# Attention and two MLPs on one core: Q loaded in one transfer per tile, two V tiles issued by ScalarE, another order, last flips in halves

## The chip, the cores and the metric

The kernel runs on one core of one Trainium2 chip. The metric is the device time of one execution in microseconds. PE is TensorE, DVE is VectorE, ACT is ScalarE, POOL is GpSimd, and SP is SyncE, which here only issues transfers. A transfer issued by SP or by ACT is an instruction in that engine's own queue.

## What is computed

Chunked attention with memory keys, then two MLPs, all in float32, each product of the MLPs split in a high and a low part so that it takes three matmuls:

```python
# q, k, v: batch 4, 8 heads, 768 positions, 64 wide; chunks of 32, left 16, right 8, 8 memory keys
for c in range(nc):
    k_full = np.concatenate([mem_k, k_ctx], axis=2)
    v_full = np.concatenate([mem_v, v_ctx], axis=2)
    scores = scale * np.matmul(q_c, k_full.transpose(0, 1, 3, 2))
    scores = scores - np.max(scores, axis=-1, keepdims=True)
    a = np.exp(scores)
    a = a / (np.sum(a, axis=-1, keepdims=True) + 1e-09)
    out[:, :, c_start:c_end] = np.matmul(a, v_full)
...
h = x @ w_in;  g = softplus(h);                                x = g @ w_out      # 3072 x 512, 2048 wide
h = x @ w_in;  g = np.maximum(h, 0) + alpha * np.minimum(h, 0); y = g @ w_out     # the second MLP
```

The weights of both MLPs arrive as doubles and are made float32 on the chip.

## The kernel before

There are 24 attention tiles of 128 tokens. A tile t goes through these steps, named as the planner names them: load Q and K (`load_q`, `load_k`) and V (`load_v`, six transfers); order Q by chunk on ACT (`qo`, `qp`, function `a_order`); copy the memory keys on POOL (`km`); scores on PE (`s`); maximum on DVE (`m`); subtract it (`c`, function `a_shift`) and exponential on ACT (`e`); sum, reciprocal on DVE (`n`, `r`); multiply by the reciprocal (`w`, on POOL for the first tiles); transpose on PE (`t`); copy the turned tile on ACT (`pt`); values on PE (`v*`); high and low half of x on ACT and DVE (`xh`, `xl`). Four tiles make one block of 512 tokens.

The first MLP goes over the six blocks in segments; one step of it is `h` (12 matmuls into `ps_hh`), softplus, high and low half, `out` (12 matmuls into `ps_o`). A pair of raw weight tiles per column group is loaded (`raw`, three buffers), made float32 by five DVE operations (`ab`, `cl`, `ca`, `cb`, `cv`), and split on ACT and POOL or DVE (`wh`, `wl`). The second MLP works on three pairs of blocks by a scheme of seven products (`quad`, `second`); its results are turned by DVE in 32x32 blocks and stored (`flip`), the very last quarter by PE (`ending`, `turn`).

The order of everything up to the second MLP comes from `Plan`: pieces with an engine, a length, a due time and what they come after. `schedule` adds the pieces; the table `O` holds offsets of the due times and switches; the plan of eight rounds that ends first by its own lengths is written out, so that each engine's queue is fixed when the program is built. `keep_busy` puts matmuls on a tile of zeros ahead of those PE pieces for which the plan sees PE idle.

In the kernel before each of the first eight tiles takes Q in two transfers, one for each half of the partitions, and only the halves of the rows that hold data; the other halves of the target (`s_room`) are set to zero by `others` (piece `qz`, four memsets, on POOL, for tile 0 on DVE). All V are issued by SP. Two lines set this:

```python
sp.dma_start(out=raw_q[t][part].rearrange("p (n k) -> p n k", k=D), in_=rows)        # load_q, for e in 0, 1
(dve.tensor_copy if other else act.copy)(out=own(q_t[t], e), in_=raw_q[t][e * D:(e + 1) * D]...)   # a_order
```

Two forms of the shifted exponential stand in the kernel already: `a_shift` with `a_exp` (DVE subtracts 512 columns, ACT takes one exponential of 512), and `a_bias` with `a_shifted_exp` (DVE scales the 8 maxima, ACT takes eight exponentials of 64 columns, each with its own bias). The switches `ca0` (tiles 0 to 3) and `ca1` (tiles 4 to 7) choose the second when they are above 0.5.

Of the kernel before, what the change touches and what calls it, by code (L numbers as in the profile page):

```python
# [31 lines left out]
QN = 2 * NPAIR * P  # L32
# [48 lines left out]

PLAN = []
RUNS = 8
O = {'qo': 19.43, 'km': 103.61, 's': 132.4, 'm': 86.98, 'c': -51.87, 'e': 175.6, 'n': -19.49, 'r': -46.35, 'w': -19.52, 't': 95.77, 'pt': 85.42, 'v': 4.11, 'xh': -85.13, 'xl': -37.52, 'first': 4.43, 'gap': 13.49, 'second': 13.8, 'gap2': 10.89, 'raw': 76.14, 'ab': -97.97, 'cl': -24.77, 'ca': -41.63, 'cb': -28.14, 'cc': -52.39, 'wh': 1.69, 'wl': -37.29, 'odd': 61.8, 'sp': 29.0, 'hi': -84.66, 'lo': 120.66, 'out': 14.22, 'wait': 0.06, 'sloads': 10.35, 'qo0': 31.77, 'qo1': 59.63, 'km0': 45.44, 'km1': -1.09, 's0': 33.53, 's1': 68.06, 'm0': 99.26, 'm1': -29.86, 'c0': 87.42, 'c1': 86.99, 'e0': -47.46, 'e1': 46.23, 'n0': 20.17, 'n1': -4.91, 'r0': 23.19, 'r1': -6.49, 'w0': -81.15, 'w1': -23.28, 't0': 107.79, 't1': -40.96, 'pt0': 0.74, 'pt1': -5.53, 'v0': -87.68, 'v1': 71.52, 'xh0': -18.53, 'xh1': -22.32, 'xl0': 2.53, 'xl1': 34.49, 'by0': 3.34, 'by1': 1.01, 'va': -80.0, 'vb': -248.8, 'vc': -188.24, 'vd': -121.62, 'ra': -92.44, 'rb': -99.39, 'rc': -59.46, 'wld': -3.93, 'dra': -16.84, 'qpd': -4.87, 'ca0': 0.43, 'ca1': -2.85}


class Plan:
# [16 lines left out]
    def run(self):  # L104
# [10 lines left out]
        while left:  # L115
            able, first = [], 1e9
            for name, since in ready.items():
                engine, us, due, _, _, take, _, _ = left[name]
                t = max(since, free.get(engine, 0.0) if engine else 0.0, now)
                if engine == "SP":  # L120
                    t = max(t, free.get("DMA", 0.0) - 4.0)
                for r in set(take):
                    short = take.count(r) - rooms[r]
                    if short > 0:
                        later = sorted(u for u, g in back if g == r)
                        t = max(t, later[short - 1] + self.LAG if len(later) >= short else 1e9)
# [24 lines left out]
            for u, g in [x for x in back if x[0] <= t]:  # L151
                rooms[g] += 1
                back.remove((u, g))
            if tab and tab != table:
                us, table = us + 1.3, tab
            if engine == "PE":
                if self.beside(name) and self.beside(last_pe):
                    us -= 0.24
                last_pe = name
                if t < 90.0 and t - free.get("PE", 0.0) > 0.5:  # L160
                    self.idle[name] = (max(free.get("PE", 0.0), came), t)
            if engine == "DVE" and free.get("POOL", 0.0) > t:
                us += 0.25 * min(us, free["POOL"] - t)
# [13 lines left out]
def attention_mlp_mlp_kernel(ctx: ExitStack, tc, qk, v, w1, w2, consts, out):  # L177
# [605 lines left out]
    def second(p, todo):  # L783
# [34 lines left out]
        for n in range(7 * NQ):  # L818
# [88 lines left out]
    def schedule(when):  # L907
# [5 lines left out]
        def nothing():  # L913
            pass

        def dma(name, issue, move, due, work, after=(), take=(), give=(), eng="SP"):
            add(("i",) + name, eng, issue, due, work, after, take)
            add(("x",) + name, "DMA", move, due, nothing, [("i",) + name])
            add(name, "", 2.0, due, nothing, [("x",) + name], [], give)

        for n, k in enumerate(order):
            f = k // 2
# [12 lines left out]
        for i, (b, f, first, final) in enumerate(steps):  # L935
# [10 lines left out]
            if final:  # L946
# [5 lines left out]
                for m in range(4):  # L952
                    by_act = m % 2 == 0 or f < HALF and O["dra"] > 0.5
                    add(("dr", i, m), "ACT" if by_act else "DVE", 0.65, t + 12.6, lambda i=i, m=m, b=b, by_act=by_act: drain_one(0 if by_act else 1, acc[b][m], staged[i][:, m, :]), [("db", i)], [], ["acc"])
                    dma(("dd", i, m), 1.1 if adds else 0.4, 1.0 if adds else 0.8, t + 16, lambda i=i, m=m, b=b, adds=adds: drain_to(m, staged[i][:, m, :], b, adds),
                        [("dr", i, m)], eng="POOL" if adds else "SP")
                add(("ds", i), "", 0.0, 0, nothing, [("dd", i, m) for m in range(4)], [], room if f < HALF else [])


# [6 lines left out]
        def tile(t, prev, due, step=None):  # L966
# [214 lines left out]
```

## Time and profile before

| | us |
|---|---|
| median of 3 runs (lowest, highest) | 1090.9 (1090.0, 1092.84) |
| the profiled execution | 1089.11 |
| its span | 1087.1 |
| PE busy | 1066.3 (98%) |
| DVE, ACT, POOL busy | 717.6, 559.7, 232.9 |

The profiled execution stands 1.8 us below the median. PE is busy through nearly all of the span, but busy time counts the matmuls on zeros too (43 of them, all before 65 us), and the matmuls of the first 72 us are spread between waits. After 72 us PE waits once, for 0.7 us, until the end of the last product at 1081 us; then come the last turns and stores.

### The profile page before, as it was taken

The numbers are of one execution on the slowest core, as the hardware profiler recorded it, in microseconds if no ns is written. First come the engines' busy times: TensorE is split into PE (matmuls) and PEld (weight loads), VectorE is DVE, ScalarE is ACT, GpSimd is POOL, SyncE is SP. The second block draws the span as 40 slices with busy tenths as digits, with TensorE's granted clock in tenths as the row PEclk, the third lists the DMA queues.
The fourth block names the chain that finished last, engine by engine and source line by source line (L and its number), as shares of the span: only waits on it lengthen the run. The fifth ranks groups of instructions, "written<-read, shape, count | busy, mean of one in ns | idle before, by whom it ended". The sixth has DMA issues, their size and how long they took to land.

```text
span 1087.1 us, 16452 instructions
## 1 busy us (share of the span) xinstructions
PE 1066.3 (98%) x6003; PEld 874.6 (80%) x6003; DVE 717.6 (66%) x1150; ACT 559.7 (51%) x974; POOL 232.9 (21%) x281
## 2 busy tenths in 40 slices
PE   7799999999999999999999999999999999999998
PEld 4578878888888888888888888888888888888886
DVE  6799989566644544444358166778666779666976
ACT  5654335465563554353244355765455665456543
POOL 4444444424123332223233400000000000000000
PEclk9899999999999999999999999999999999999999
DMA  9955674768644465444356373799874999856904
GB/s 225 234 152 185 167 187 121 187 164 215 186 127 151 153 197 137 167 118 151 111 194 225 134 304 113 293 276 318 201 275 174 335 300 255 239 223 252 370 1 78
DMA packets 173839, 214.53 MB, mean 197 GB/s; under 512 B 96064, under 2 KB 125888, under 8 KB 166848
## 3 DMA queue, kind: packets, MB, share of 16 engines
q1 hardware_dynamic: 169456, 196.59, 56.6%
q0 software_dynamic: 4032, 16.78, 7.9%
q8 instruction: 47, 0.77, 0.3%
q14 instruction: 32, 0.26, 0.1%
q10 hardware_dynamic: 272, 0.13, 0.0%
HBM read 154.74 MB, written 46.14 MB: 185 GB/s over the span
## 4 chain that ended last, share of the span: by engine, by line
PE 94%; DVE 3%; DMA 2%; SPq 1%; ACT 0%; issue 0%; DVEq 0%; ACTq 0%
PE ps_q L71 41%; PE ps_o L71 24%; PE ps_hh L71 24%; PE ps_x L71 2%; PE ps_s L71 2%; DVE word L71 1%; DMA raw<-in_w_dram 1%; PE ps_t L71 1%; SPq L71 1%; DMA wout<-out_ops 1%; DMA qk<-in_qk_dram 0%; DVE sm L71 0%; DVE x L71 0%; DVE nm L71 0%; DVE v L71 0%
## 5 line engine op out<-in xcount | busy, mean ns | idle before, releaser
L71 PE MATMUL ps_hh<-x,wsplit 128*128 128x512 f32 x1152 | 280.2, 392 | 0.6 <-DVE x L71 0.5
L71 PE MATMUL ps_o<-g,wsplit 128*128 128x512 f32 x1152 | 279.4, 391 | 0.8 <-ACT ta L71 0.7
L71 PEld LDWEIGHTS ps_o<-g,wsplit 128*128 128x128 f32 x1152 | 215.0, 188 | 46.5 <-ACT ta L71 1.1
L71 PEld LDWEIGHTS ps_hh<-x,wsplit 128*128 128x128 f32 x1152 | 214.5, 188 | 45.7 <-DVE x L71 0.8
L71 PE MATMUL ps_q<-g,wout 128*128 128x512 f32 x1008 | 229.3, 389 | 0.1
L71 PE MATMUL ps_q<-xop,win 128*128 128x512 f32 x1008 | 229.2, 389 | 0.0
L71 PEld LDWEIGHTS ps_q<-g,wout 128*128 128x128 f32 x1008 | 189.1, 188 | 39.8 <-ACT gb L71 0.5
L71 PEld LDWEIGHTS ps_q<-xop,win 128*128 128x128 f32 x1008 | 189.2, 188 | 39.4
L71 DVE TENSOR_TENSOR g<-ta,g 128x512 fp32r<-128x512 f32 x96 | 71.8, 748 | 132.3 <-ACT g L71 132.1
L71 ACT CAST g<-gb 128x512 fp32r<-128x512 f32 x168 | 100.8, 622 | 88.5 <-PE ps_q L71 64.6
L71 DVE TENSOR_TENSOR g<-gb,g 128x512 fp32r<-128x512 f32 x168 | 114.3, 687 | 37.9 <-ACT g L71 36.2
L71 ACT CAST g<-ta 128x512 fp32r<-128x512 f32 x96 | 59.6, 621 | 147.8 <-PE ps_o L71 147.6
L71 ACT ACTIVATE ta<-ps_hh 128x512 f32<-128x512 f32 x96 | 57.4, 598 | 106.3 <-PE ps_hh L71 101.9
L71 DVE SCALAR_TENSOR_TENSOR word<-raw,word 128x512 int32<-128x512 int32 x128 | 106.3, 831 | 2.5
L71 ACT ACTIVATE tp<-gb 128x512 f32<-128x512 f32 x48 | 30.4, 633 | 91.8 <-DVE gb L71 91.8
L71 POOL TENSOR_TENSOR wst<-wsum,wst 128x512 fp32r<-128x512 f32 x32 | 42.3, 1321 | 124.6 <-ACT wst L71 124.6
L71 POOL DMA_DIRECT2D gb<-gb x12 | 10.5, 874 | 263.6 <-DVE g L71 176.1
L71 DVE TENSOR_SCALAR word<-word 128x512 f32<-128x512 f32 (+1 forms) x128 | 65.0, 512 | 1.8
L71 POOL TENSOR_TENSOR wsplit<-word,wsplit 128x512 fp32r<-128x512 f32 x32 | 48.9, 1531 | 64.7 <-ACT wsplit L71 58.1
L71 DVE SCALAR_TENSOR_TENSOR gb<-gb,tp 128x512 f32<-128x512 f32 x48 | 33.2, 692 | 44.0 <-ACT tp L71 44.0
L71 POOL TENSOR_TENSOR wst<-word,wst 128x512 fp32r<-128x512 f32 (+1 forms) x32 | 37.6, 1176 | 110.7 <-ACT wst L71 110.7
L71 DVE TENSOR_SCALAR word<-raw 128x512 int32<-128x512 int32 x64 | 39.0, 610 | 32.0 <-POOL wst L71 13.6
(81 smaller groups left out, 930.9 us busy)
## 6 DMA issues: line engine op xcount, KB each, us to landing
wout<-out_ops SPq DMA_DIRECT2D x42, 1024.0 KB
raw<-in_w_dram SPq DMA_DIRECT2D x64, 512.0 KB
win<-in_ops SPq DMA_DIRECT2D x24, 1024.0 KB
win<-in_ops SPq DMA_DIRECT2D x24, 768.0 KB
out_ops<-wst SPq DMA_DIRECT2D x56, 256.0 KB
in_ops<-wst SPq DMA_DIRECT2D x24, 512.0 KB
gb<-gb POOLq DMA_DIRECT2D x12, 1024.0 KB, 13.5
v<-in_v_dram SPq DMA_DIRECT2D x48, 128.0 KB
```

Of the source, the lines that this page charges most:

```text
L71: i = getattr(self.engine, name)(*args, **kw)
```

## The change

Q of the first eight tiles comes in one transfer of 128 rows of 4 KB, zeros included (the host's layout holds them), so the memsets `qz` are gone; `a_order` copies all 128 partitions for one chunk at a time. `load_v` takes a queue, and the switches `vq0` and `vq4` put V of tiles 0 and 4 on ACT's queue. The table `O` is another one throughout (cut below to the switches that change what is done: `ca0` is now on, `wld` puts the low halves of the first two weight tiles on DVE, all `by` stay on). `Plan` weighs DVE, PE and accumulating transfers a little differently, which moves pieces but is no work. The flip of the quarter (0, 0) of each pair comes at steps 50 and 51, one half at each, where both halves came at step 53; the other two flips stay at steps 39 and 46.

```diff
-O = {... 'wld': -3.93, 'dra': -16.84, 'qpd': -4.87, 'ca0': 0.43, 'ca1': -2.85}
+O = {... 'wld': 2, 'dra': 0, 'qpd': 0, 'ca0': 1, 'ca1': 0, 'vq0': 1, 'vq1': 0, 'vq2': 0, 'vq3': 0, 'vq4': 1, 'vq5': 0, 'vq6': 0, 'vq7': 0, 've': 70.11}
...
-            raw_q[t] = room[:, :QN // 2]
+            raw_q[t] = room[:, :QN]
...
         if c is None:
-            sp.dma_start(out=raw_q[t][part].rearrange("p (n k) -> p n k", k=D), in_=rows)
+            sp.dma_start(out=raw_q[t], in_=qk[t][:, :QN])
...
-    def load_v(t):
+    def load_v(t, queue):
...
-            sp.dma_start(out=v_t[t][to:to + n, part], in_=v[t][at:at + n, part])
+            queue.dma_start(out=v_t[t][to:to + n, part], in_=v[t][at:at + n, part])
 
     def a_order(t, e, other=False):
-        (dve.tensor_copy if other else act.copy)(out=own(q_t[t], e), in_=raw_q[t][e * D:(e + 1) * D].rearrange("p (n c k) -> p c n k", c=2, k=CHUNK))
+        (dve.tensor_copy if other else act.copy)(out=q_t[t][:, e], in_=raw_q[t].rearrange("p (n c k) -> p c n k", c=2, k=CHUNK)[:, e])
...
-            if (i, q) in ((4, 7), (5, 6), (6, 5)):
-                d, b = ((0, 1), (1, 1), (0, 0))[i - 4]
-                flip(c.pop((d, b)), 2 * p + b, d)
+            for at, half, d, b in ((39, 0, 0, 1), (39, 1, 0, 1), (46, 0, 1, 1), (46, 1, 1, 1), (50, 0, 0, 0), (51, 1, 0, 0)):
+                if n == at:
+                    flip(c[d, b], 2 * p + b, d, [half])
...
-                add(("qz", t), "POOL" if t else "DVE", 1.5 if t else 1.1, (-50, 0)[t > 0] + t, lambda: others(q_t[t], pool if t else dve), [("vr", t)])
```

The order. First place: the head of ACT's queue. `v_119`, `v_117` hold tile 0's V and ordered Q, `qk_97` to `qk_100` tiles 0 to 3's Q and K; DMAHW0 to 7 are eight semaphores that the transfers of SP and ACT take in turn, so that a transfer waits in its queue until the one that held its semaphore before has landed. Before:

```order
L71 ACT_TABLE_LOAD
L71 COPY v_119<-qk_97 64x16x32 [waits DMAHW0_49]
L71 COPY v_119<-qk_97 64x16x32 [waits DMAHW1_49]
L71 COPY v_171<-qk_98 64x16x32 [waits DMAHW3_49]
L71 ACTIVATE v_119<-v_119 128x512 [waits DVE_49,PE_49]
L71 COPY v_171<-qk_98 64x16x32 [waits DMAHW4_49]
```

And in the changed kernel:

```order
L71 DMA v_117<-in_v_dram 8x512
L71 DMA v_117<-in_v_dram 56x512
L71 DMA v_117<-in_v_dram 64x512
L71 DMA v_117<-in_v_dram 64x512 [waits DMAHW1_49]
L71 DMA v_117<-in_v_dram 56x512 [waits DMAHW3_49]
L71 DMA v_117<-in_v_dram 8x512 [waits DMAHW5_49]
L71 ACT_TABLE_LOAD
L71 COPY v_117<-qk_97 128x512 [waits DMAHW0_49]
L71 COPY v_117<-qk_97 128x512
L71 COPY v_129<-qk_98 128x512 [waits DMAHW2_49]
L71 COPY v_129<-qk_98 128x512
L71 ACTIVATE v_117<-ps_s,nm 128x64 [waits DVE_49,PE_49,Activation_49]
```

The six transfers of V now stand ahead of everything that ACT does; the fourth waits for DMAHW1, which tile 0's K (`qk_97`, 128x4x160) holds, the fifth and sixth for V's own first and second piece.

Second place: SP's queue behind the V of tile 3 (`v_255`, in the changed kernel `v_216`). Before, tile 4's Q and K (`qk_340`) and V (`v_357`) follow, then tile 5's Q (`qk_358`):

```order
L71 DMA v_255<-in_v_dram 56x512 [waits DMAHW6_49]
L71 DMA v_255<-in_v_dram 8x512 [waits DMAHW7_49]
L71 DMA qk_340<-in_qk_dram 64x8x64 [waits DMAHW0_49]
L71 DMA qk_340<-in_qk_dram 64x8x64 [waits DMAHW1_49]
L71 DMA qk_340<-in_qk_dram 128x4x160 [waits DMAHW2_49]
L71 DMA v_357<-in_v_dram 8x512 [waits DMAHW3_49]
```

In the changed kernel two weight tiles come first, the second of which (the fourth in all) waits for DVE to free one of the three raw buffers, and Q and K of tiles 4 to 7 follow without V:

```order
L71 DMA raw<-in_w_dram 128x512 [waits DMAHW3_49]
L71 DMA raw<-in_w_dram 128x512 [waits DMAHW4_49,DVE_49]
L71 DMA qk_392<-in_qk_dram 128x1024 [waits DMAHW5_49]
L71 DMA qk_392<-in_qk_dram 128x4x160 [waits DMAHW6_49]
L71 DMA qk_421<-in_qk_dram 128x1024 [waits DMAHW7_49]
L71 DMA qk_421<-in_qk_dram 128x4x160 [waits DMAHW0_49]
L71 DMA qk_441<-in_qk_dram 128x1024 [waits DMAHW2_49]
```

Third place: ACT behind the turned copy of tile 2 (`pt`). Before, weights (`wsplit`), x of tile 2 and Q of tile 4 follow:

```order
L71 COPY pt<-ps_t 64x8x32 x3
L71 CAST wsplit<-word 128x512 [waits DVE_49]
L71 CAST x<-ps_x 128x4x128 [waits PE_49]
L71 COPY v_357<-qk_340 64x16x32 [waits DMAHW0_49]
L71 COPY pt_95<-ps_t 64x8x32 [waits PE_49,Activation_49]
L71 COPY pt_95<-ps_t 64x8x32 [waits Activation_49] x3
```

In the changed kernel tile 3's exponentials and tile 4's V stand ahead of x of tile 2 and of everything of tile 3 behind its exponential:

```order
L71 CAST wsplit<-word 128x512 [waits DVE_49]
L71 ACTIVATE v_216<-ps_s,nm 128x64 x7
L71 DMA v_422<-in_v_dram 8x512 [waits DMAHW1_49]
L71 DMA v_422<-in_v_dram 56x512 [waits DMAHW3_49]
L71 DMA v_422<-in_v_dram 64x512 [waits DMAHW5_49]
L71 DMA v_422<-in_v_dram 64x512 [waits DMAHW7_49]
L71 DMA v_422<-in_v_dram 56x512 [waits DMAHW1_49]
L71 DMA v_422<-in_v_dram 8x512 [waits DMAHW3_49]
L71 CAST wsplit<-word 128x512 [waits DVE_49]
L71 CAST x<-ps_x 128x4x128 [waits PE_49]
L71 COPY pt_95<-ps_t 64x8x32 [waits PE_49]
```

Here DMAHW5 was last taken by Q of tile 4 (`qk_392`, 128x1024) and DMAHW7 by Q of tile 5 (`qk_421`, 128x1024).

## Rows read from the trace of the kernel before

**Rows 1.** Windows: length, PE, PEld, DVE, ACT, POOL busy (instructions), PEclk, DMA share, GB/s.

```profile
20.00:30.00 10.00, 7.60 (x93) 4.55 (x89) 9.86 (x20) 6.19 (x14) 5.65 (x11) 1.00 0.93 264
...
40.00:50.00 10.00, 6.34 (x74) 5.30 (x73) 7.15 (x17) 6.08 (x11) 1.98 (x4) 0.66 0.97 243
...
200.00:300.00 100.00, 100.00 (x724) 82.81 (x723) 60.06 (x98) 54.78 (x93) 34.43 (x44) 1.00 0.72 191
```

**Rows 2.** Waits of PE from 72 us on: in total, times, longest.

```profile
PE ps_o L71 <- ACT ta L71: 0.7, 1, 0.7
```

**Rows 3.** The chain that ended last, near 83 us: start, length, what.

```profile
83.02 2.72 PE ps_hh L71 x12
```

**Rows 4.** PE in order of time: start, length, operation, [idle before <- releaser].

```profile
1.01 4.84 PE L71 MATMUL ps_s<-zero 128*128 128x512 bf16 x11 [1.01 <-POOL zero L71]
6.51 1.17 PE L71 MATMUL ps_s<-qk,v 128*64 128x64 f32 x32 [0.67 <-POOL qk L71]
...
34.20 2.83 PE L71 MATMUL ps_hh<-x,wsplit 128*128 128x512 f32 x11 [0.54 <-DVE x L71]
...
44.47 1.11 PE L71 MATMUL ps_t<-cst,v 128*128 128x128 f32 x4 [3.39 <-POOL v L71]
45.86 1.98 PE L71 MATMUL ps_s<-qk,v 128*64 128x64 f32 x32 [0.27 <-DVE v L71]
47.59 1.95 PE L71 MATMUL ps_x<-pt,v 128*64 128x64 f32 x32
...
55.33 0.60 PE L71 MATMUL ps_t<-cst,v 128*128 128x128 f32 x4
...
58.63 1.15 PE L71 MATMUL ps_x<-pt,v 128*64 128x64 f32 x32
```

**Rows 5.** SP's queue in the opening: start, time to issue, transfers.

```profile
0.75 4.06 SPq L71 DMA_DIRECT2D qk<-in_qk_dram  x6
...
9.66 3.04 SPq L71 DMA_DIRECT2D v<-in_v_dram  x6
...
25.38 2.21 SPq L71 DMA_DIRECT2D qk<-in_qk_dram  x3
```

**Rows 6.** ACT in the opening, columns as rows 4.

```profile
0.75 1.28 ACT L71 ACT_TABLE_LOAD   x1 [0.75 <-PEq L1171]
3.82 0.62 ACT L71 COPY v<-qk 64x512 f32<-64x512 f32 x1 [1.79 <-DMA qk<-in_qk_dram]
...
15.19 1.51 ACT L71 COPY pt<-ps_t 64x256 f32<-64x256 f32 x4 [3.12 <-PE ps_t L71]
```

**Rows 7.** POOL in the opening, columns as rows 4.

```profile
6.25 0.36 POOL L71 COPY qk<-qk 128x32 f32<-128x32 f32 x2 [4.21 <-DMA qk<-in_qk_dram]
```

**Rows 8.** DVE in the opening, columns as rows 4.

```profile
18.18 0.43 DVE L71 TENSOR_SCALAR word<-raw 128x512 int32<-128x512 int32 x1 [0.20 <-DMA raw<-in_w_dram]
18.52 0.68 DVE L71 TENSOR_REDUCE sm<-v 128x8 f32<-128x512 f32 x1
...
22.31 0.20 DVE L71 RECIPROCAL r<-sm 128x8 f32<-128x8 f32 x1
...
24.42 0.67 DVE L71 SCALAR_TENSOR_TENSOR word<-raw,word 128x512 int32<-128x512 int32 x1
```

**Rows 9.** Short windows, columns as rows 1: Q alone, then weights alone.

```profile
2.50:3.00 0.50, 0.50 (x2) 0.15 (x1) 0.41 (x2) 0.00 (x0) 0.00 (x0) 1.00 0.87 198
...
64.00:65.00 1.00, 1.00 (x12) 0.61 (x9) 0.17 (x1) 0.79 (x2) 1.00 (x1) 1.00 0.94 385
```

**Rows 10.** SP's queue at the end, columns as rows 5.

```profile
1078.64 4.15 SPq L71 DMA_DIRECT2D out_dram<-c  x8
1082.89 1.05 SPq L71 DMA_DIRECT2D out_dram<-o_sb  x2
```

**Rows 11.** ACT at the end: its copies, then its one transfer.

```profile
1081.89 0.89 ACT L71 COPY o_sb<-ps_q 128x512 f32<-128x512 f32 x2 [4.74 <-PE ps_q L71]
1082.81 0.49 ACTq L71 DMA_DIRECT2D out_dram<-o_sb  x1
```

More of the change, by code (lines that the diff above doesn't have):

```diff
@@ L83 @@
 RUNS = 8
-O = {'qo': 19.43, 'km': 103.61, 's': 132.4, 'm': 86.98, 'c': -51.87, 'e': 175.6, 'n': -19.49, 'r': -46.35, 'w': -19.52, 't': 95.77, 'pt': 85.42, 'v': 4.11, 'xh': -85.13, 'xl': -37.52, 'first': 4.43, 'gap': 13.49, 'second': 13.8, 'gap2': 10.89, 'raw': 76.14, 'ab': -97.97, 'cl': -24.77, 'ca': -41.63, 'cb': -28.14, 'cc': -52.39, 'wh': 1.69, 'wl': -37.29, 'odd': 61.8, 'sp': 29.0, 'hi': -84.66, 'lo': 120.66, 'out': 14.22, 'wait': 0.06, 'sloads': 10.35, 'qo0': 31.77, 'qo1': 59.63, 'km0': 45.44, 'km1': -1.09, 's0': 33.53, 's1': 68.06, 'm0': 99.26, 'm1': -29.86, 'c0': 87.42, 'c1': 86.99, 'e0': -47.46, 'e1': 46.23, 'n0': 20.17, 'n1': -4.91, 'r0': 23.19, 'r1': -6.49, 'w0': -81.15, 'w1': -23.28, 't0': 107.79, 't1': -40.96, 'pt0': 0.74, 'pt1': -5.53, 'v0': -87.68, 'v1': 71.52, 'xh0': -18.53, 'xh1': -22.32, 'xl0': 2.53, 'xl1': 34.49, 'by0': 3.34, 'by1': 1.01, 'va': -80.0, 'vb': -248.8, 'vc': -188.24, 'vd': -121.62, 'ra': -92.44, 'rb': -99.39, 'rc': -59.46, 'wld': -3.93, 'dra': -16.84, 'qpd': -4.87, 'ca0': 0.43, 'ca1': -2.85}
+O = {'qo': 30.33, 'km': 84.14, 's': 91.95, 'm': 109.26, 'c': -17.61, 'e': 178.31, 'n': -17.92, 'r': -11.95, 'w': -78.56, 't': 180.11, 'pt': 161.35, 'v': 22.95, 'xh': -41.96, 'xl': 4.27, 'first': 21.85, 'gap': 34.28, 'second': 0.0, 'gap2': 0.83, 'raw': 107.43, 'ab': -164.05, 'cl': 0.38, 'ca': -84.0, 'cb': -2.76, 'cc': -13.13, 'wh': -66.22, 'wl': -41.75, 'odd': 77.78, 'sp': 86.94, 'hi': -161.87, 'lo': 79.15, 'out': 7.77, 'wait': 0.1, 'sloads': 35.53, 'qo0': -11.74, 'qo1': 136.15, 'km0': 35.59, 'km1': 41.17, 's0': 26.73, 's1': 74.58, 'm0': 133.68, 'm1': -93.99, 'c0': 162.97, 'c1': 149.24, 'e0': -109.85, 'e1': 67.1, 'n0': 14.44, 'n1': -56.97, 'r0': -9.69, 'r1': 13.43, 'w0': -135.29, 'w1': -76.5, 't0': 138.51, 't1': -5.69, 'pt0': -54.64, 'pt1': 57.94, 'v0': -156.16, 'v1': 16.61, 'xh0': -36.76, 'xh1': -159.4, 'xl0': -11.13, 'xl1': 106.59, 'by0': 1, 'by1': 1, 'va': -84.93, 'vb': -183.48, 'vc': -136.3, 'vd': -247.55, 'ra': -159.88, 'rb': -94.86, 'rc': -102.4, 'wld': 2, 'dra': 0, 'qpd': 0, 'ca0': 1, 'ca1': 0, 'vq0': 1, 'vq1': 0, 'vq2': 0, 'vq3': 0, 'vq4': 1, 'vq5': 0, 'vq6': 0, 'vq7': 0, 've': 70.11}
 class Plan:
@@ L159, in run @@
                 last_pe = name
+                if t > 90.0 and t - free.get("PE", 0.0) > 2.0:
+                    us += 1.6
                 if t < 90.0 and t - free.get("PE", 0.0) > 0.5:
                     self.idle[name] = (max(free.get("PE", 0.0), came), t)
-            if engine == "DVE" and free.get("POOL", 0.0) > t:
-                us += 0.25 * min(us, free["POOL"] - t)
+            if engine == "DVE":
+                us *= 0.88
+                if free.get("POOL", 0.0) > t:
+                    us += 0.3 * min(us, free["POOL"] - t)
             done[name] = t + us
@@ L767, in ending, with flip @@
             turn(c[:, 1, part], 1, 2 * h, 2, (lambda o, i: act.copy(out=o, in_=i), dve.tensor_copy)[h], (act, sp)[h])
-    def flip(c, b, d):
+    def flip(c, b, d, halves=range(2)):
         rows = out[b * N2:(b + 1) * N2, d * HK:(d + 1) * HK].rearrange("(c i) (m a j) -> m a i c j", i=32, m=2, j=32)
-        for m in range(2):
+        for m in halves:
             o = c[:, m, :].rearrange("p (c i) -> p c i", i=32)
@@ L914, in nothing, with dma @@
             pass
-        def dma(name, issue, move, due, work, after=(), take=(), give=(), eng="SP"):
+        def dma(name, issue, move, due, work, after=(), take=(), give=(), eng="SP", land=2.0):
             add(("i",) + name, eng, issue, due, work, after, take)
             add(("x",) + name, "DMA", move, due, nothing, [("i",) + name])
-            add(name, "", 2.0, due, nothing, [("x",) + name], [], give)
+            add(name, "", land, due, nothing, [("x",) + name], [], give)
         for n, k in enumerate(order):
@@ L954, in schedule @@
                     add(("dr", i, m), "ACT" if by_act else "DVE", 0.65, t + 12.6, lambda i=i, m=m, b=b, by_act=by_act: drain_one(0 if by_act else 1, acc[b][m], staged[i][:, m, :]), [("db", i)], [], ["acc"])
-                    dma(("dd", i, m), 1.1 if adds else 0.4, 1.0 if adds else 0.8, t + 16, lambda i=i, m=m, b=b, adds=adds: drain_to(m, staged[i][:, m, :], b, adds),
-                        [("dr", i, m)], eng="POOL" if adds else "SP")
+                    dma(("dd", i, m), 1.2 if adds else 0.4, 2.2 if adds else 0.8, t + 16, lambda i=i, m=m, b=b, adds=adds: drain_to(m, staged[i][:, m, :], b, adds),
+                        [("dr", i, m)], eng="POOL" if adds else "SP", land=4.0 if adds else 2.0)
                 add(("ds", i), "", 0.0, 0, nothing, [("dd", i, m) for m in range(4)], [], room if f < HALF else [])
@@ L981, in load @@
             def load(c=None):
-                for e in range(2):
+                for e in range(2 if few else 1):
                     load_q(t, e, c)
@@ L987, in tile @@
             else:
-                dma(("qk", t, 2), 1.45, 2.7, soon, lambda: (load(), load_k(t)), [("qr", t)])
+                dma(("qk", t, 2), 1.2, 2.9, soon, lambda: (load(), load_k(t)), [("qr", t)])
             kafter = [("i", "q", t, 1)]
@@ L992, in tile @@
             add(("vr", t), "", 0.0, soon + 2, lambda: room_v(t), [("i", "qk", t, 2)] + ([("i", "v", prev)] if prev >= 0 else []), vrooms)
-            dma(("v", t), 2.9, 2.0, (O["va"], O["vb"], O["vc"], O["vd"])[t] if start else due - 24, lambda: load_v(t), [("vr", t)])
+            by_act = not few and O["vq%d" % t] > 0.5
+            dma(("v", t), 3.0, 2.0, (O["va"], O["vb"], O["vc"], O["vd"])[t] if start else due - (24 if few else O["ve"]), lambda: load_v(t, act if by_act else sp), [("vr", t)], eng="ACT" if by_act else "SP")
             queries = [("q", t, c) for c in range(2) if few or c]
             if not few:
-                add(("qz", t), "POOL" if t else "DVE", 1.5 if t else 1.1, (-50, 0)[t > 0] + t, lambda: others(q_t[t], pool if t else dve), [("vr", t)])
-                add(("qo", t), "ACT", 0.6, due - when_due("qo"), lambda: a_order(t, 0), [("qk", t, 2), ("qz", t)])
+                add(("qo", t), "ACT", 0.6, due - when_due("qo"), lambda: a_order(t, 0), [("qk", t, 2), ("vr", t)])
                 other = start and O["qpd"] > 0.5
-                add(("qp", t), "DVE" if other else "ACT", 0.5 if other else 0.6, due - when_due("qo"), lambda: a_order(t, 1, other), [("qo", t)])
+                add(("qp", t), "DVE" if other else "ACT", 0.7 if other else 0.6, due - when_due("qo"), lambda: a_order(t, 1, other), [("qo", t)])
                 queries = [("qp", t)]
```

## The prediction, written before the changed kernel ran

> **What bounds the kernel now.** I read the windows first, then PE's waits, then PE, ACT, POOL, DVE and SP in order of time. From 72 us on PE waits once, for 0.7 us [rows 2], and a stage such as 200 to 300 us is full of matmuls [rows 1]. Nothing off PE can be won there. What can move is when PE gets there. I use a mark: by 83.02 us [rows 3] the kernel before has finished the scores, transposes and values of tiles 0 to 7 and ten products of the first MLP (six `h`, four `out`), each 2.72 us [rows 3]. The changed order has the same PE work behind it after seven `h` and three `out`. If the mark comes x us later, the end does too, as long as the rest stays full.
>
> Up to the mark PE is not full: it waits 3.39 us for POOL before 44.47 [rows 4], and the mean granted clock from 40 to 50 us is 0.66 [rows 1], that is, the lower level, 1.2 GHz, for much of it, after that wait. A score step takes 1.98 us there and 1.17 at 2.4 GHz, a transpose 1.11 and 0.60, values 1.95 and 1.15 [rows 4]. The transfers are as full as PE is not: DMA share 0.93 and 0.97 [rows 1]. So the opening is a race between loads and a chain of ACT, DVE and POOL steps, and the first `h` at 34.20 [rows 4] is where it is read.
>
> **Transfers of Q.** Before, a tile's Q is 262 KB in short rows; such a stretch moved 198 GB/s [rows 9], 1.3 us. Now it is 524 KB in rows of 4 KB; weights in rows of that length moved 385 GB/s [rows 9], 1.4 us. I take 1.4: twice the bytes in about the same time. The far bound is the mean of a mixed stretch, 264 [rows 1]: 2.0 us. SP issues one transfer less, some 0.7 us per tile (three took 2.21 [rows 5], the last of them K).
>
> **The memsets** of POOL and DVE go. In PE's waits for POOL they stand behind the scores of tile 1; what they give is covered by step 1 below, which is later. I count nothing. The shift of tiles 0 to 3 leaves DVE (one tensor operation of about 0.7) for ACT: eight exponentials of 64 columns for one of 512. Nothing in the trace is that small on ACT; four copies of 256 columns took 1.51, 0.38 each, one of 512 took 0.62 [rows 6], and the line through them gives 0.20, 1.6 us a tile (1.2 if the fixed part is smaller, 2.0 if the bias adds).
>
> **Two V on ACT.** SP needs 3.04 us to issue a V [rows 5]. If SP's issuing were the limit, two V less would free 6.1 us. But the share of the DMA engines in that stretch is 0.93 to 0.97 [rows 1], so the bytes are the limit and I count no gain. The Trainium skill, "DMA: Bandwidth & Descriptors", section "Issuing engines are not separate DMA queues", says the same against the change: transfers started by several engines run on the same 16 DMA engines, and only issue time is saved. By that rule the move is worth at most those 6.1 us and here nothing; the DMA share agrees.
>
> What the move costs is ACT. A transfer in ACT's queue holds ACT until its semaphore is free, and behind it stand the table load and every copy. The trace of before has no such wait, so I walk through the order.
>
> *Step 1, the head.* ACT's fourth piece of V waits for tile 0's K. K landed by 6.25 before [rows 7]. Ahead of it now are 0.1 us more of Q and the first three pieces of V, 262 KB at 264 GB/s [rows 1], 1.0 us: 7.3 (6.3 if V gets no share, 8.3 if all 524 KB more go at 264). Three issues at 0.49 [rows 11] make 8.8, the table load 1.28 and two copies of 0.62 [rows 6] make 11.3, the scores 1.17 make 12.5. PE's filler ends at 5.85 [rows 4] and nothing follows until about 11, so I expect the lower level, 0.8 more: 13.3, where before it was 7.68.
>
> *Step 2, tiles 0 to 2.* Maximum 0.68 and scaling 0.20 [rows 8] bring the first exponential to 14.3. From there ACT runs nearly without a break: 1.6, Q of tile 2 1.24, 1.6, turned copy 1.51, half of Q of tile 3 0.62, 1.6, and 0.5 of waiting for the transpose: 23.0. DVE then has a sum 0.68, a low half of x 0.7, scaling and reciprocal 0.20 each: 24.8. Only then comes the first weight tile's conversion, three operations of 0.43 and two of 0.67 [rows 8]: 27.4. It frees the raw buffer for the fourth weight tile, and **Q and K of tiles 4 to 7 stand behind that transfer on SP**. Tile 4's Q, issued at 25.38 before [rows 5], goes out at 27.8.
>
> *Step 3, tile 4's V.* ACT's fourth piece waits for tile 5's Q. From issue at 0.75 [rows 5] to ACT's copy at 3.82 [rows 6] the first half of Q took 3.07 us, of which 0.7 was moving 131 KB at 198: 2.4 fixed. In front are a weight tile and two Q at 385, 4.1 us, a K of 328 KB at 264, 1.2, and three pieces of V, 1.0: it lands at 36.1 (38.0 with everything at 264). Three issues: 37.6. Before, ACT waited for no load of this kind.
>
> *Step 4, the first `h`.* ACT: weights and x of tile 2, 1.24; turned copy of tile 3, 1.51; Q of tile 4, 1.24; weights and half a Q, 1.24; high half of x of tile 3, 0.6; DVE's low half 0.7, behind another operation of 0.7: 44.8, **10.6 us later** than 34.20.
>
> *Step 5, from there to the mark.* By then the scores of tiles 4 and 5 are done. Left: ten products 27.2, two scores 2.3, four transposes 2.4, four values 4.6, together 36.5 at 2.4 GHz, if PE is full: the weights are converted, V of tiles 5 to 7 are issued from about 41 on, and DVE, 9.86 of 10 busy in rows 1, has spent its idle time earlier. That gives 81.3. The kernel before needs 48.8 us for its part, since it waits. PE again idled before 39 us, so one transpose, score and values cost up to 2.1 more [rows 4]; half of it lies under ACT's copies of step 4: 1.0. These sums leave out the hand-overs between engines: POOL's first copy of two ends at 6.43 [rows 7] and PE begins at 6.51 [rows 4], 0.08. For some twenty I add 1.5. The mark is at 83.8, **0.8 us late**.
>
> **The halves of the last flip.** SP issues the last eight stores of `c` until 1082.79 and the two turned results right behind, though the first copy that they wait for began at 1081.89 and took about 0.6 [rows 10, 11]. Two to three steps earlier (six matmuls each, half a product, 1.36 us) SP is free: 0.4 us gained (0 if the last store's landing sets the end anyway, 1.0 if its bytes also wait less). DVE's two transposes fall between its low halves for PE, which the code asks for three steps ahead (`asked`), 4 us; that covers them, and without it each would cost PE its own length.
>
> **Sum.** 1089.11 + 0.8 - 0.4 = 1089.5 against the profiled execution; the median of before stands 1.8 above it, so 1091.3. Within 0.3% (3.3 us either way, about what a measurement of this kernel can tell from no change) is 1087.6 to 1094.2, and that is this case's own range. Chance 0.54.
>
> **Rival: ACT isn't held.** If tile 4's and 5's Q have landed when ACT comes to tile 4's V, that costs only six issues, 2.9 us. ACT comes there at about 30.6 (23.0, then 0.6, 1.51, 0.62, 0.6, 1.51, 0.62, 1.6 and 0.5 of waits) and leaves at 33.5 instead of 37.6: 4.1 us won. If the head isn't held either, another 4 us at the first score, of which the loads give back half: 1091.3 - 6.1 = 1085.2. For it speaks that SP needs only some 2 us to issue Q and K of tiles 4 and 5; against it that 1.6 MB and more would have to move in the 3 us behind the fourth weight tile. Decides: tile 5's Q landed before 31 us. Chance 0.20.
>
> **Rival, slower: long rows go no faster than the mix.** If Q moves at 264 and not 385 GB/s, eight tiles take 4.8 us more of a full DMA stretch: 0.7 at the head, 1.3 in step 3, and the rest on tiles 6 and 7 and the V behind them, before which PE would wait. With a PE that waits for those in full (1.5 of the remaining 2.8) and the other half of the low clock in step 5 (1.0) it makes 4.5: 1095.8. The point from which it is slower than 0.3% is about 290 GB/s. For it: K, Q, V and weights lie mixed in these queues, and the mixed mean is 264. Chance 0.26.
>
> **Chances and range.** Faster by over 0.3%: 0.20, within: 0.54, slower: 0.26, the three cases. Half of each rival lies outside 1086 to 1096, under 0.2 together.
>
> **What would show it.** Right: ACT's first copy of Q near 10 us, a wait of ACT on a load of Q ending near 36, the first `h` near 45, and PE full from there to the mark near 83.8. Wrong: the first `h` before 40 (ACT not held), PE waits between 45 and 83 of over 2 us (loads late), or waits of over 1 us after 90, which no step here has.

## The result, and the profile after

The changed kernel takes 1096.7 us (median of 6, 1095.6 to 1097.5) where the kernel before took 1090.95 in the same session (median of 6): a ratio of 1.0051, interval 1.004 to 1.0062, 5.7 us slower. The prediction of 1091.3 and its range to 1096 were too low. The profiled execution is 1095.6 us long, its span 1093.8.

Up to the mark the prediction held; the loss lies behind it. First the head and the middle of ACT's opening in the changed kernel (start, length, operation, [idle before <- releaser]); rows 6 show the head before:

```profile
0.74 7.18 ACTq L71 DMA_DIRECT2D v<-in_v_dram  x6
7.96 1.28 ACT L71 ACT_TABLE_LOAD   x1 [7.96 <-DMA v<-in_v_dram]
9.26 2.18 ACT L71 COPY v<-qk 128x512 f32<-128x512 f32 x4
...
33.36 4.81 ACTq L71 DMA_DIRECT2D v<-in_v_dram  x4
38.20 0.62 ACT L71 CAST wsplit<-word 128x512 fp32r<-128x512 f32 x1 [5.91 <-DMA v<-in_v_dram]
```

ACT issues V of tile 0 until 7.92 and the last four pieces of tile 4's V until 38.17, and nothing of its own runs meanwhile. PE of the changed kernel, same columns; the counterparts before are rows 4:

```profile
40.01 1.98 PE L71 MATMUL ps_x<-pt,v 128*64 128x64 f32 x32 [3.39 <-ACT pt L71]
...
45.70 3.37 PE L71 MATMUL ps_hh<-x,wsplit 128*128 128x512 f32 x12
...
83.69 2.88 PE L71 MATMUL ps_o<-g,wsplit 128*128 128x512 f32 x12
86.42 2.88 PE L71 MATMUL ps_hh<-x,wsplit 128*128 128x512 f32 x12
...
108.98 2.88 PE L71 MATMUL ps_hh<-x,wsplit 128*128 128x512 f32 x12
114.31 4.58 PE L71 MATMUL ps_o<-g,wsplit 128*128 128x512 f32 x12 [2.44 <-DVE o_sb L71]
...
138.65 2.97 PE L71 MATMUL ps_o<-g,wsplit 128*128 128x512 f32 x12 [0.68 <-DVE o_sb L71]
```

The mark of the kernel before, in the same columns:

```profile
82.86 2.88 PE L71 MATMUL ps_hh<-x,wsplit 128*128 128x512 f32 x12
```

The first `h` starts at 45.70 and the mark (seven `h`, three `out` done) is at 83.69, 0.8 behind the kernel before, where it is at 82.86 in this view and 83.02 in rows 3. The product that starts at 138.65 is the 19th from the mark on; eighteen products at 2.72 are 49.0 us, and here they took 55.0. So of the 6.5 us between the two profiled executions 0.8 come up to the mark and 6.0 behind it; the kernel before has one wait of 0.7 further on, at 152 us, that the changed kernel doesn't have. PE's waits from 72 us on, in total, times, longest; rows 2 had 0.7 in one wait:

```profile
PE ps_o L71 <- DVE o_sb L71: 3.6, 3, 2.4
```

The waits are for DVE's copies of `ps_o` (the odd `dr` pieces), which free the accumulator banks; behind the longest of them the next 12 matmuls took 4.58 instead of 2.88, 1.7 more, at a granted clock of 0.79 from 114 to 116 us and 0.57 from 116 to 119. Together with the waits that is 5.3 of the 6.0 us. Three windows (0 to 80, 80 to 84, 84 to 140), columns as rows 1, first of the kernel before, a stretch that rows 1 left out:

```profile
0.00:80.00 80.00, 64.59 (x695) 47.24 (x696) 61.97 (x120) 47.69 (x88) 35.20 (x72) 0.94 0.79 207
80.00:84.00 4.00, 4.00 (x20) 3.30 (x19) 4.00 (x8) 1.82 (x4) 1.35 (x1) 1.00 0.41 131
84.00:140.00 56.00, 55.87 (x247) 45.99 (x246) 55.69 (x83) 22.35 (x40) 25.70 (x18) 1.00 0.62 179
```

and of the changed kernel:

```profile
0.00:80.00 80.00, 65.14 (x686) 47.92 (x691) 57.62 (x115) 49.64 (x115) 22.12 (x42) 0.89 0.81 226
80.00:84.00 4.00, 4.00 (x20) 3.30 (x19) 3.97 (x6) 1.63 (x4) 4.00 (x2) 1.00 0.83 228
84.00:140.00 56.00, 52.36 (x222) 42.24 (x221) 55.24 (x84) 21.32 (x37) 21.67 (x17) 0.97 0.54 164
```

DVE (third pair) was busy 55.69 of 56 us in the kernel before already, beside a PE that was full by itself: two engines at their limit at once, with no slack for DVE. The chain by line between 40 and 139 us changes accordingly, first before, then after:

```profile
by line: PE ps_hh L71 39.9%; PE ps_o L71 36.2%; DMA raw<-in_w_dram 5.1%; PE ps_x L71 4.3%; DVE word L71 3.3%; DVE sm L71 3.1%; PE ps_t L71 2.6%; PE ps_s L71 2.0%; ACT pt L71 1.5%; DVE nm L71 1.4%; issue 1.3%; DVE v L71 1.3%; DVE r L71 0.6%;
```

```profile
by line: DVE word L71 59.0%; issue 13.7%; DVE g L71 7.5%; PE ps_hh L71 5.8%; DVE o_sb L71 2.6%; DVE x L71 2.5%; PE ps_s L71 2.2%; ACT pt L71 1.5%; DVE sm L71 1.5%; DVE nm L71 1.1%; ACT wsplit L71 0.6%; DVE v L71 0.6%; ACT x L71 0.6%; PE ps_
```

From 76% matmuls to 59% weight conversions (`word`). In DVE's fixed order 57, 85, 112 and 139 `word` operations stood ahead of the first four pairs of drains before; in the changed kernel it is 60, 90, 120 and 143. DVE's first drains of the first three pairs start at 89.08, 113.48 and 137.82 in the changed kernel: 30 `word` operations and what stands between them take 24.3 to 24.4 us, where eight products take PE 21.8. Before, with 28 and 27, they start at 83.90, 106.81 and 128.38, 22.9 and 21.6 apart.

### The profile page after: what moved, and what is told of

Same layout as the page of the kernel before. It is cut to its first block, busy times and chain, and to the rows that moved or that the text cites. A ratio compares the mean times of both kernels' runs of the same rounds, so it can differ in the third digit from the quotient of the medians.

```text
span 1093.8 us, 16380 instructions
## 1 busy us (share of the span) xinstructions
PE 1070.5 (98%) x5998; PEld 877.1 (80%) x6002; DVE 720.7 (66%) x1148; ACT 563.2 (51%) x1002; POOL 224.4 (21%) x251
## 4 chain that ended last, share of the span: by engine, by line
PE 86%; DVE 9%; DMA 2%; issue 2%; ACT 1%; SPq 0%; ACTq 0%; POOL 0%; DVEq 0%
PE ps_q L71 42%; PE ps_o L71 20%; PE ps_hh L71 20%; DVE word L71 6%; PE ps_s L71 2%; PE ps_x L71 2%; DMA qk<-in_qk_dram 1%; DVE g L71 1%; PE ps_t L71 1%; ACT v L71 0%; DMA raw<-in_w_dram 0%; DVE sm L71 0%; DVE xop L71 0%; DVE x L71 0%; DVE o_sb L71 0%
## 5 line engine op out<-in xcount | busy, mean ns | idle before, releaser
L71 DVE TENSOR_TENSOR g<-ta,g 128x512 fp32r<-128x512 f32 x96 | 75.5, 786 | 145.0 <-ACT g L71 145.0
L71 POOL TENSOR_TENSOR wst<-wsum,wst 128x512 fp32r<-128x512 f32 x32 | 44.7, 1398 | 128.0 <-ACT wst L71 118.8
L71 DVE TENSOR_SCALAR word<-word 128x512 int32<-128x512 int32 (+1 forms) x128 | 67.2, 528 | 2.1
L71 POOL TENSOR_TENSOR wsplit<-word,wsplit 128x512 fp32r<-128x512 f32 x30 | 44.9, 1500 | 69.8 <-ACT wsplit L71 69.8
L71 DVE TENSOR_SCALAR word<-raw 128x512 int32<-128x512 int32 x64 | 36.2, 565 | 30.0 <-POOL wst L71 14.2
```

What stands on the lines that cost most here:

```text
L71: i = getattr(self.engine, name)(*args, **kw)
```

## The experiments

Two theories. **A:** ACT, held twice by V, starves DVE in the opening (busy for 62.0 us by 80 us before, 57.6 after, some of it work that the change removed), and DVE, which has no slack later, is late at the drains. **B:** the new order puts more conversions ahead of the drains than DVE can do in the time, hold or no hold. Ratios are against the kernel before on the same chip; "mark" and "19th" are the starts of the two products above, from each run's PE timeline, for the kernels with the new order.

| run | median us | ratio (interval) | mark | 19th | between |
|---|---|---|---|---|---|
| after | 1096.7 | 1.0051 (1.004 to 1.0062) | 83.69 | 138.65 | 54.96 |
| e1 V on SP | 1092.5 | 1.0021 (1.0008 to 1.0033) | 78.59 | 133.63 | 55.04 |
| e9 V of tile 4 on SP | 1093.2 | 1.0024 (1.0013 to 1.0035) | 81.46 | 136.59 | 55.13 |
| e10 V of tile 0 on SP | 1099.6 | 1.0079 (1.0064 to 1.0094) | 86.00 | 140.86 | 54.86 |
| e2 drains on ACT | 1094.1 | 1.0036 (1.0022 to 1.005) | 83.41 | 134.43 | 51.02 |
| e5 drains sooner | 1094.0 | 1.0025 (1.0014 to 1.0035) | 84.79 | 135.71 | 50.92 |
| e6 sooner, V on SP | 1090.7 | 0.9995 (0.9982 to 1.0008) | 80.18 | 131.32 | 51.14 |
| e7 fewer clamps, V on SP | 1086.9 | 0.9961 (0.9946 to 0.9975) | 81.53 | 131.55 | 50.02 |
| e11 drains on ACT, V on SP | 1087.7 | 0.9971 (0.996 to 0.9983) | 81.03 | 130.01 | 48.98 |
| e3 before, V on ACT | 1094.2 | 1.0043 (1.0031 to 1.0055) | | | |
| e4 before, Q only | 1090.3 | 1.0005 (0.9991 to 1.0019) | | | |
| e8 before, fewer clamps | 1088.0 | 0.9969 (0.9957 to 0.998) | | | |
| e12 before, drains on ACT | 1088.4 | 0.9975 (0.996 to 0.999) | | | |
| e13 before, new price | 1100.9 | 1.0105 (1.0086 to 1.0124) | | | |
| e14 old price | 1098.0 | 1.0069 (1.0053 to 1.0085) | | | |
| e15 old price, V on SP | 1096.5 | 1.0058 (1.0041 to 1.0076) | | | |

### The hold of ACT: e1, e3, e9, e10

All keep the order and move only the queue that issues V:

```diff
-lambda: load_v(t, act if by_act else sp)
+lambda: load_v(t, sp)                              # e1
+lambda: load_v(t, act if t == 0 else sp)           # e9
+lambda: load_v(t, act if t == TB else sp)          # e10
+lambda: load_v(t, act if t in (0, TB) else sp)     # e3, in the kernel before
```

> The changed kernel, its order kept, with both V (tiles 0 and 4) issued by SP at the same place of the program. Theory A (ACT's two waits starve VectorE in the opening, and VectorE, full from 80 us on, is late ever after): the first h comes 5 us or more earlier than 45.7, PE's three waits for o_sb copies of VectorE (3.6 us) go, and the time is 1089 to 1092. Theory B (the new order asks VectorE for more conversions ahead of each drain than it can do in the time: 60, 90 and 120 word operations stand ahead of the first three pairs of drains where 57, 85 and 112 stood before): the first h is earlier too, but the waits for o_sb stay, or at the most the first goes, and the time is 1094 to 1096.

> The kernel before, its order kept, with V of tiles 0 and 4 issued by ACT at the same place of the program. Theory A: ACT is held as in the changed kernel, VectorE is late at 84 us, PE waits for o_sb behind it, 1094 to 1097. Theory B: ACT is held in the opening, but the drains of before stand behind fewer conversions, so that it costs 2 us at the most: 1090 to 1093.

> The changed kernel, its order kept, with V of tile 4 alone issued by SP (V of tile 0 stays on ACT). Both V on SP brought some 4 us. If the hold at 33 to 38 us, just ahead of the first weights' high halves, is the larger part: 1093 to 1094.5, first h 3 to 5 us before 45.7. If the head's hold (the first 7 us) is: 1095 to 1097.

> The same with V of tile 0 alone issued by SP (V of tile 4 stays on ACT). The complement: 1095 to 1096.5 if tile 4's hold is the larger part, 1092.5 to 1094 if the head's is. If the first h of the two come at gains that add up to 6 us, the holds add; if each alone brings less than half, one hides the other.

Without the hold (e1) the first `h` starts at 39.53, 6.2 earlier, and the mark is 5.1 earlier. PE's waits for the drains do not go, they grow from 3.6 to 5.3; from 72 us on in e1:

```profile
PE ps_o L71 <- DVE o_sb L71: 5.3, 3, 2.4
```

The product behind e1's wait of 2.40 takes 3.01 at a granted clock of 1.00, where the changed kernel's took 4.58; the eighteen products take 55.04 in e1 and 54.96 in the changed kernel. So the low clock adds nothing of its own, as far as these two profiles go: without it the waits are longer, and DVE's drains set the time either way. The time, 1092.5, lies between the two ranges that I gave.

In e3 the hold alone is put into the kernel before: the mark comes at 88.17 instead of 82.86 and DVE's first drain at 89.2 instead of 83.9, and nothing waits for it. Its window from 84 to 140 us, then PE's only wait from 72 to 200:

```profile
84.00:140.00 56.00, 55.86 (x247) 45.96 (x246) 55.73 (x84) 22.56 (x39) 25.68 (x17) 1.00 0.58 172
```

```profile
PE ps_o L71 <- ACT ta L71: 0.7, 1, 0.7
```

So A is right that the hold costs time (after to e1: 0.0030 of 1091, 3.3 us; e3: 4.7), and wrong that it makes the waits. The time of e3 lies in A's range, 1094 to 1097, but by a later mark and not by the waits that A named. The column "between" says it most plainly: 55 us in four kernels whose marks lie from 78.6 to 86.0.

It is tile 4's V that holds. Alone on SP (e9) it brings nearly all that both bring (1.0024 against 1.0021). Tile 0's V alone on SP (e10) makes it worse: ACT reaches tile 4's V at 29.56, some 1.5 us sooner than in the changed kernel, and is held for 11 us instead of 5.9. ACT in e10:

```profile
29.56 10.84 ACTq L71 DMA_DIRECT2D v<-in_v_dram  x6
40.44 0.62 ACT L71 CAST wsplit<-word 128x512 fp32r<-128x512 f32 x1 [10.96 <-DMA v<-in_v_dram]
```

ACT goes on at 40.4, later than in the changed kernel (38.2), so coming earlier to the hold gains nothing. My expectation for e10 missed by 3 us. The hold ends 2.2 us later, though SP issues Q of tile 4 sooner (27.57 instead of 28.89): the first of the six issues takes 4.05 us there (29.56 to 33.61) and 0.28 in the changed kernel, and the fifth, which waits for the semaphore of the first transfer, goes out at 38.95 instead of 37.23, the sixth at 40.12 instead of 37.85. Why the first one takes 4.05 stays open.

### The place of the drains: e2, e5, e6, e11

e2 changes the engine of DVE's drains in the first eight segments. e5 and e6 emit `db` and DVE's two drains right behind the `out` that fills the banks (55, 85, 115 and 138 `word` operations ahead of them), e6 with V on SP. e11 has V on SP, all four drains of the first four segments on ACT, and holds back ACT's `wh` and POOL's `wl` between that `out` and the drains:

```diff
-by_act=by_act: drain_one(0 if by_act else 1, ...
+by_act=by_act: drain_one(0 if by_act or i < 32 else 1, ...          # e2; e11: i < 16
...
+    sooner = {("out", i): [("db", i), ("dr", i, 1), ("dr", i, 3)] for i in (3, 7, 11, 15)}     # e5, e6
```

> The changed kernel with all copies of ps_o to o_sb in the first eight drains (to about 190 us) on ACT instead of half of them on VectorE, order kept. A and B: PE no longer waits for o_sb on VectorE, no stretch at the low clock near 114, the product that starts at 138.65 comes some 5 us earlier, and the time is 1091 to 1092. Rival C (the drains are only where the time shows; VectorE's low halves g stand in the same queue and PE waits for those next): the waits move to g, and the time stays above 1094.5.

> The changed kernel (V of tiles 0 and 4 on ACT) with VectorE's copies of the first four drains right behind the product that fills them: 55, 85, 115 and 138 word operations stand ahead of them instead of 60, 90, 120 and 143. Nothing else moves. Theory B (order): PE's waits for o_sb (3.6 us) and the low clock behind them (1.7 us) go, the mark stays at 83.7, and the time is 1091 to 1093. Theory A (VectorE is late by what it lost in the opening, whatever stands where): the waits move to the low halves or the weights on VectorE, 1095 to 1097.

> As the run with V of tiles 0 and 4 on SP, and VectorE's copies of the first four drains right behind the product that fills them. If the hold of ACT and the place of the drains are two separate causes: the mark as in that run (its fourth out starts at 78.6), its 5.3 us of waits for o_sb under 1.5, and the time 1086.5 to 1088.5, faster than before. If VectorE is simply too slow for a PE that comes earlier: the waits go elsewhere, 1090.5 to 1092.5.

> As the run with V of tiles 0 and 4 on SP, with all four copies of each of the first four drains on ACT, and ACT's high halves of the weights that the order puts between a drain's product and the drain (and POOL's low halves behind them) right behind the drain. VectorE loses eight copies of 0.6 us before 150 us, and no drain stands behind a conversion or behind a copy that waits for one. If VectorE's throughput is the bound up to 150 us and the drains only its visible end: waits under 1.5 us, 1086 to 1088, faster than both. If ACT's drains wait as they did when only their engine was changed (1.8 us at 134): 1089.5 to 1091.

Five `word` operations fewer ahead of the drains take the price up to the 19th product from 6.0 to 2.0 and 2.2 us (e5, e6); in e6 1.5 more follow in the middle of that product. Neither time is in the range that I gave for the order as the cause: e5's 1094.0 lies between its two ranges, and e6's 1090.7 in the one for a DVE that is simply too slow. PE's waits from 72 to 200 us in e6:

```profile
PE ps_o L71 <- DVE o_sb L71: 1.9, 1, 1.9
PE ps_o L71 <- ACT o_sb L71: 1.5, 1, 1.5
```

The hold is worth the same with and without that edit (e5 to e6: 0.0030, after to e1: 0.0030), so the two add up as separate causes do; what e6 has left are drains that are late all the same. In e2 ACT's own drain comes late once (a wait of 1.8), because ACT stands at a `wsplit` copy that waits 2.70 us for DVE's `word` ahead of it, and the product behind that wait takes 4.61 instead of 2.88: 2.0 of the 6.0 us stay up to the 19th product and 1.7 in it. So e2 gains 1.6 us (0.0015), a third of what A and B said. e11 takes that away too. Its window from 84 to 140:

```profile
84.00:140.00 56.00, 56.00 (x249) 46.34 (x248) 52.58 (x83) 25.70 (x47) 22.92 (x18) 1.00 0.63 181
```

PE is full and DVE has 3.4 us to spare. At 1087.7 us it is faster than both kernels, by 0.3% (0.17% to 0.4%) than the one before.

### DVE as the bound: e7, e8, e12

The clamp is left out in the conversions 8 to 23 (e7 with V on SP, e8 in the kernel before); e12 is the kernel before with e11's edit of the drains.

```diff
-lambda k=k: clamp(0, k, dve)
+lambda k=k, n=n: clamp(0, k, dve) if not 8 <= n < 24 else None
```

> As the run with V of tiles 0 and 4 on SP, and without the clamp of the weights in conversions 8 to 23 (it leaves that part of the computation out), so VectorE has 16 operations of 0.42 us less between about 65 and 140 us, order kept. If VectorE's throughput is the bound there: the 5.3 us of waits for o_sb fall below 1, and the time is 1086.5 to 1088.5. If it isn't: unchanged, 1091.5 to 1093.

> Control: the kernel before without the clamp of the weights in conversions 8 to 23 (it leaves that part of the computation out). VectorE is as full there (55.7 of 56 us from 84 to 140), but PE doesn't wait for it, so the time stays within 1 us of before, with VectorE less busy.

> The kernel before with that same edit of the drains. Leaving out 16 clamps gave it 3 us, so VectorE is its bound too, though PE shows no wait for o_sb there: 4.8 us less of copies on VectorE, part of them behind the stretch that counts, bring 1 to 2.5 us, 1088.5 to 1090. If its 3 us came from the opening alone (the clamps before 84 us): 1090.5 to 1091.5.

In e7 the order is e1's and only DVE's load is less; PE's waits from 72 to 200 us fall from 5.3 to 0.5 and the kernel gains some 6 us (5.6 by the medians, 0.0060 by the ratios):

```profile
PE ps_o L71 <- DVE o_sb L71: 0.5, 2, 0.3
```

The bound is DVE's throughput; the drains are its visible end. e8 was meant as a control and missed: the kernel before gains 3.0 us although PE showed no wait for DVE in the later stretch. Its four-engine window there now has DVE at 47.45 of 56; its mark is at 81.02 instead of 82.86, by the same view, but one execution doesn't fix a mark: e12, with the same order up to there as the kernel before, has it at 84.68, and three kernels with the opening of the changed one and no hold (e1, e6, e11) have it between 78.59 and 81.03. What doesn't depend on that is the stretch behind the mark. The 27th product from the mark on starts here before, then in e8:

```profile
154.94 2.88 PE L71 MATMUL ps_hh<-x,wsplit 128*128 128x512 f32 x12
```

```profile
151.74 2.88 PE L71 MATMUL ps_hh<-x,wsplit 128*128 128x512 f32 x12
```

The 26 products up to there take 72.1 us in the kernel before, and 70.7 in e8, which is 26 times 2.72. In e12, which gains 2.3 us without leaving anything out, they take 70.7 too (84.68 to 155.40), and in e3, with the hold, 72.1 again (88.17 to 160.28). So 1.4 us of either gain lie there: the kernel before lost them to a late DVE already, though the view of the waits puts them down to ACT's `ta` (0.7, at 152 us) or shows none. The rest of e8's gain, and of e12's, which no single execution can place, stays open.

### The planner's price of DVE: e13, e14, e15

The planner now takes 0.88 of each DVE operation's length (and 0.3 instead of 0.25 of it more beside POOL). e13 puts that price into the kernel before; e14 and e15 take it out of the changed kernel, e15 with V on SP. The order is planned anew each time.

```diff
-            if engine == "DVE" and free.get("POOL", 0.0) > t:
-                us += 0.25 * min(us, free["POOL"] - t)
+            if engine == "DVE":
+                us *= 0.88
+                if free.get("POOL", 0.0) > t:
+                    us += 0.3 * min(us, free["POOL"] - t)
```

> The kernel before, its table kept, with the planner's new price of VectorE (0.88 of an operation's length, and 0.3 of it more beside POOL) and so the order that follows from it: 66, 95, 124 and 150 word operations ahead of the first four pairs of drains, where it had 57, 85, 112 and 139. If the price is what puts work that is not yet due ahead of the drains: PE waits for o_sb, 9 to 12 operations of 0.7 to 0.8 us late, less what the opening gains: 1093 to 1098. If the table matters and the price doesn't: within 1.5 us of before.

> The changed kernel, its table kept, with the planner's old price of VectorE and the order that follows: 54, 83, 110 and 132 word operations ahead of the drains. V of tiles 0 and 4 stay on ACT, so ACT is held as before. If the price is the cause of the waits: no wait for o_sb on VectorE over 1 us, the mark not earlier than 83.7 (the hold stays), 1091 to 1094. If not: 1096 or more.

> The same with both V issued by SP: both causes taken out. 1087 to 1090, below before; 1091 or more if a third cause remains.

With the new price the kernel before gets the waits of the changed one. PE's waits from 72 to 200 us in e13:

```profile
PE ps_o L71 <- DVE o_sb L71: 3.9, 2, 2.0
PE ps_hh L71 <- DVE x L71: 0.2, 1, 0.2
```

With the old price these waits are gone; what is left in e15:

```profile
PE ps_o L71 <- POOL wsplit L71: 0.4, 1, 0.4
```

So it is the price that puts conversions ahead of the drains. The times of e14 and e15 missed what I expected by 4 us and more: the table was made for the other price, and the plan that follows has its first `h` at 50.5 and 45.7 and PE busy for only 96.8 and 96.3 of the 100 us from 200 to 300, where the changed kernel is full. e13's loss of 11 us is more than its waits, and above the range that I gave (1093 to 1098): seven `h` and three `out` are done at 88.44, 5.6 later than before, and the eighteen products from there take 53.7 us, 4.7 more than 49.0, so half of the loss lies ahead of the drains. These runs settle where the waits come from, not what a table made for the old price would give.

## Why the prediction was wrong, step by step

- **Transfers of Q: right.** Windows of the changed kernel between 31 and 38 us, with Q of tiles 4 to 7 under way, moved 321 to 391 GB/s; e4 (Q in one transfer and no memsets, alone, in the kernel before) is at 1.0005. The slower rival's mechanism, long rows at 264 GB/s, is not there.

> The kernel before, its order kept, with Q of tiles 0 to 7 in one transfer of 4 KB rows each and without the zeroing, and nothing else. If Q moves at some 350 to 385 GB/s in long rows: as much DMA time as before, SP's queue 0.7 us a tile shorter, 1089 to 1091.5. If it moves at the mean of a mixed stretch (264 GB/s): 1094 to 1096.

- **Two V on ACT: right in kind, and in size in part by luck.** The walk through ACT's queue gave 37.6 for the end of tile 4's V (measured 38.2), 44.8 for the first `h` (45.7), 83.8 for the mark (83.7). The first `h` came 0.9 late and the way from there to the mark took 38.0 where the sum had 39.0, so two misses cancel, and marks after the same opening differ by more than a microsecond (83.41 in e2, 84.79 in e5). The 34.20 that I read as the first `h` of before is its second matmul; the first starts at 33.17. The kernels without the hold have their mark 2.2 to 5.1 earlier. What the trace of before could not show, the walk through the order with durations of its rows did.
- **"If the mark comes x us later, the end does too, as long as the rest stays full": the failed step.** The condition broke. I took a window of 200 to 300 us for "the rest", where DVE is 60% busy, and an opening window of 20 to 30 where it is full, and concluded that DVE "has spent its idle time earlier". The windows from 84 to 140 us, of the same view, show DVE at 55.69 of 56, and the window from 100 to 150, which stood in the same answer as rows 1, shows it at 49.73 of 50. The new order asks DVE for 3, 5 and 8 more `word` operations by the first three pairs of drains; 69 of them took 52.0 us from 84 to 140 us, 0.75 each. By my estimate 8 at 0.75 are 6.0 us, and 6.0 were lost behind the mark, against the 0 in my sum.
- **The planner's weights.** I described them as moving pieces without being work, and looked for what they move only up to the mark, at the heads of ACT and SP. The order of DVE's queue at the first four drains, 57 to 60 and 112 to 120, was there to be counted.
- **The last flip: right, a little smaller.** From the first last turn to the end of the span it is 5.84 to 5.97 us in five kernels with the old flip (before, e3, e8, e12, e13) and 5.48 to 5.53 in nine with the new one (e1, e2, e5, e6, e7, e9, e10, e14, e15): 0.4 won. The profiled execution of the changed kernel, at 6.02, is one in which it didn't show; e11 (6.27) and e4, with the old flip (6.98), are two more of that sort.
- **Wrong if:** the last of the signs named, waits of over 1 us after 90, is what came.

## What to carry to other kernels

When an engine off the critical path is as busy as the critical one in some stretch, a change of order can make it the bound at no cost of work: read the windows of every stretch that lies behind the change, not of one that stands for the rest, and count in each queue what now stands ahead of an operation that frees a buffer for the critical engine. A transfer that an in-order compute engine issues holds everything behind it until its semaphore is free (here ACT stood for 5.9 us, and for 11.0 in e10); look which transfer held that semaphore and when it lands. Cheaper prices in a planner are a change of the order at every place where that engine is full.

## What the hardware showed

DVE and POOL hold each other up. Mostly it is one DVE operation that runs beside a two-input operation of POOL and is stretched until that one ends. POOL and then DVE of the kernel before, near 80 us, columns as rows 4:

```profile
80.47 1.35 POOL L71 TENSOR_TENSOR wsplit<-word,wsplit 128x512 fp32r<-128x512 f32 x1 [2.23 <-ACT wsplit L71]
```

```profile
80.59 1.51 DVE L71 TENSOR_SCALAR word<-word 128x512 int32<-128x512 int32 x1
82.02 0.41 DVE L71 TENSOR_SCALAR word<-raw 128x512 int32<-128x512 int32 x1
```

The first operation takes 1.51 instead of 0.41 and ends 0.3 us behind POOL's. But at times POOL is the one that is held up. POOL and then DVE of the kernel before, near 90 us:

```profile
89.48 3.90 POOL L71 TENSOR_TENSOR wsplit<-word,wsplit 128x512 fp32r<-128x512 f32 x1 [2.82 <-ACT wsplit L71]
```

```profile
90.61 0.68 DVE L71 TENSOR_TENSOR g<-ta,g 128x512 fp32r<-128x512 f32 x1
91.22 0.68 DVE L71 SCALAR_TENSOR_TENSOR word<-raw,word 128x512 int32<-128x512 int32 x1
91.82 0.41 DVE L71 TENSOR_SCALAR word<-word 128x512 int32<-128x512 int32 x1
92.27 1.67 DVE L71 SCALAR_TENSOR_TENSOR word<-raw,word 128x512 int32<-128x512 int32 x1
```

Here POOL's operation takes 3.90 instead of 1.35, while the DVE operations beside it keep their 0.41 and 0.68 up to the one at 92.27; what decides which of the two waits, these rows don't show. Where DVE is the one, a low half of POOL's costs it about 1.1 us, while the planner adds 0.3 of an operation's length, 0.2 us at the most. Alone, a conversion's operations follow each other closely (82.02, then 82.36 and 82.96 in the same stretch: 0.34 and 0.60), which the price of 0.88 (0.40 and 0.62) fits. The planner's price comes to 0.49 us in the mean over a conversion's five operations; in the chip they were 0.75 long from 84 to 140 us. The Trainium skill says in "SBUF — State Buffer", section "Terms", that DVE and GpSimd share a port pair that one of them holds for a full instruction while the other blocks; the rows above agree, with 1.51 instead of 0.41 for DVE and 3.90 instead of 1.35 for POOL.
